# Two stores of a channel-attention kernel, split by partitions over two DMA queues

## The chip, the cores and the metric

The kernel runs on one core of one Trainium2 chip. The metric is the device time of one execution in microseconds. A profile is one execution taken by the hardware profiler; its span goes from the first to the last of the program's own instructions.

## What is computed

The input x is an image of 384 x 384 pixels with 384 channels in bf16 (113 MB). Each channel is averaged over the image, the average is multiplied by one weight and put through a sigmoid, and every pixel's channel is multiplied by the result:

```
g = jnp.einsum("bhwc->bc", x) / (H * W)
s = sigmoid(g * w1d[0])
return x * s[:, None, None, :]
```

So all of x must be read before the first byte of the result is known, and all of it is written. x does not fit into the core's memory: what doesn't stay has to be read twice.

## The kernel before

The pixels are dealt out as 1152 rows for each of 128 partitions; a row is one pixel's 384 channels (768 bytes) in every partition, so a row of all partitions is 96 KB. The tile `arena` holds the rows that are in the chip.

**First phase, to about 268 us.** Loads bring all rows into the arena (`load`, L235). TensorE sums each row over the partitions into one PSUM bank (`sum_rows`, `add_held`, L241 and L255). Some rows are only streamed through and are read again later. Others are kept: a few as they are, and most in groups that VectorE folds, four rows of bits into three (`fold`, `bits` L275, `join` L281), with a test by ScalarE (L312).

**The gap.** When the last row has landed and is summed, ScalarE takes the sigmoid (`s_bf`, L449) and copies it to PSUM (L453). In between, the DMA engines have nothing to do: nothing is left to load, and nothing can be stored.

**Second phase.** Rows that lie in the arena are multiplied by the scale on VectorE, three pieces of them on GpSimd (`scale`, L462), and stored (`store`, L472). The rows that were kept as they are come first, in a list: four times 2 rows at Y, four times 2 rows at T, then 6 rows at A + 26, 7 rows at A + 32, then 13 and more. Then folded groups are unfolded and scaled while streamed rows are loaded again (L235), scaled and stored. A load can start when the stores that read its place in the arena have landed.

**What sets the order.** Every DMA of x, load or store, is issued by SyncE (SP), one after the other, and SP waits at each until its turn may go. The order is written by a planner in the kernel, a loop over a model of time: it sends a store when VectorE should be through with its rows (`send`, then `waiting` and `store`), and issues a load when a large enough run of rows is idle. `Flow.add` records each step with what it reads and writes; `Flow.emit` turns that into semaphore waits (L106, L112) and gives each engine's DMAs 24 semaphores in turn (`LANES`). ScalarE's queue carries only the load of the weight. After the gap ScalarE copies rows that were parked in PSUM back into the arena (`copy_bank`, L387).

The first load after the gap fetches 21 rows into a run of the arena that starts in the rows named above, so it waits for their stores.

Of the kernel before, what the change touches and what calls it, by code (L numbers as in the profile page):

```python
# [127 lines left out]
def kernel(  # L128
# [11 lines left out]
    nc = tc.nc  # L140
    P = nc.NUM_PARTITIONS
# [18 lines left out]
    A = V + PAIR  # L160
# [27 lines left out]
    arena = pool.tile([P, ROWS, C], bf16, name="arena")  # L188
# [11 lines left out]
    of = out.rearrange("b h w c -> (b h w) c")  # L200

    def view(t, r0, n):
        return t[r0 * P : (r0 + n) * P, :].rearrange("(p r) c -> p r c", r=n)

    def rows(lo, n):
        return [("a", r) for r in range(lo, lo + n)]

    fl = Flow(nc, tc)
# [5 lines left out]
    STREAMED, KEPT = (0, N_STREAM), (N_STREAM, N_KEPT)  # L214
# [76 lines left out]
    def fold(k):  # L291
# [46 lines left out]
        reads=["ones", "w_bf"], writes=["bank0"],  # L338
# [4 lines left out]
        reads=["bank0"], writes=["w_sc"],  # L343
# [41 lines left out]
    def copy_bank(i, src, dst, reads, writes):  # L385
        fl.add(
            "ACT", lambda: nc.scalar.copy(dst.bitcast(u32), src.bitcast(u32)), reads=reads, writes=writes  # L387
        )

    for i, bk in enumerate(banks):  # L390
        lo, hi = i * BANK, min((i + 1) * BANK, PS * C)
# [51 lines left out]
    for a, n in S2 + [(U, 8)] + S3 + S1 + [(V, 8), (Y + 2, 6), (T + 6, 4), (T + 3, 3), (T + 1, 2), (T, 1)]:  # L443
# [6 lines left out]
        reads=["bank0", "w_sc"], writes=["s_bf"],  # L450
# [6 lines left out]
    def scale(a, n, eng="DVE", s=s_bf, after=()):  # L457
        v = arena[:, a : a + n, :]
        vec = nc.vector if eng == "DVE" else nc.gpsimd
        fl.add(  # L460
            eng,
            lambda: vec.tensor_tensor(  # L462
                out=v, in0=v, in1=s[:, None, :].to_broadcast([P, n, C]), op=Op.mult
            ),
            reads=rows(a, n) + ["s_bf" if s is s_bf else "bank0"], writes=rows(a, n), after=after,
        )

    def store(chunk, a, lo, hi):
        r0, n = chunk
        return fl.add(  # L470
            "SP",
            lambda: nc.sync.dma_start(out=view(of, r0, n)[:, lo:hi, :], in_=arena[:, a : a + hi - lo, :]),  # L472
            reads=rows(a, hi - lo), dma=True,
        )

    def unfold(k, first):

# [40 lines left out]
    def TT(n):  # L518
        return 0.15 + 0.2 * n
# [85 lines left out]
    def send(chunk, a, lo, hi, then, known=None):  # L605

        waiting.append((dve_at, hi - lo, then, chunk, a, lo, [] if known is None else known))

    def backlog():
        return sum(e[1] for e in moves) + ROW * sum(e[1] for e in waiting)  # L610
# [10 lines left out]
    def stored(a, n):  # L621

        def f():
            for i in range(a, a + n):
                for left in needed:
                    left.discard(("a", i))
                if not Y <= i < Y + 8 and not U <= i < U + 8 and not V <= i < V + 8:
                    idle[i] = True
        return f
# [30 lines left out]
    def start_group():  # L660

        if not line:
            return False
        g = line[0]
        column = home[g]
        if needed[column] or not free[column] or g == BANKED and (bank_at is None or now < bank_at[1]):
            return False
        line.popleft()
        free[column] = False
        a, q = GROUPS[g]  # L670
        if g == BANKED:
            a = bank_at[0]

        below = 0
        if column < 2 and g != COLUMNS[column][0]:
            below = GROUPS[COLUMNS[column][COLUMNS[column].index(g) - 1]][1]

        def part():
            release(a + below, sent - below)

        def done():
            nonlocal out_rows
            out_rows += 1
            free[column] = True
            release(a + max(below, sent), n_rows - max(below, sent))

        for k in of_group(g):
            turns.extend(step + (None,) for step in unfold(k, a))
        sent, n_rows = 0, 4 * q + (g == BANKED)
        if len(line) >= total - N_SPLIT and q == PAIR:  # L690

            f, t, _ = turns[-6]
            sent = 3 * PIECE
            turns[-6] = (f, t, lambda: send(KEPT, a, c_group[g], c_group[g] + sent, part, written))
        f, t, _ = turns[-1]
        turns[-1] = (f, t, lambda: send(KEPT, a + sent, c_group[g] + sent, c_group[g] + n_rows, done, written))
        return True

    while True:

        if dve_at <= now:
            ahead = backlog()
            can = bool(turns)
            if not can and not alongside and (ahead >= PENDING or not landed):
                can = start_group()
            if landed and (ahead < PENDING or not can):
                chunk, a, lo, n, end = landed.popleft()
                scale(a, n, s=s_ps if alongside and now else s_bf)
                dve_at = now + TT(n)
                since = (a, lo) if since is None else since  # L710
                if end or ahead < MERGE:
                    b, first = since
                    send(chunk, b, first, lo + n, stored(b, lo + n - first))
                    since = None
            elif can:
                f, t, then = turns.popleft()
                f()
                dve_at = now + t
                if then:
                    then()  # L720
        if alongside and alongside[0][0] <= now:
            _, chunk, a, lo, n = alongside.popleft()
            store(chunk, a, lo, lo + n)
            moves.append([now + LAT, n * ROW + PER_STORE, stored(a, n)])
        while waiting and waiting[0][0] <= now:
            _, n, then, chunk, a, lo, known = waiting.popleft()
            known.append(store(chunk, a, lo, lo + n))
            last_is_load = False
            moves.append([now + LAT, n * ROW + PER_STORE, then])
        if not asked and not line and not turns:  # L730
            verdict()
            asked = True
        if out_rows == total and not checked:
            checked = True
            fl.add("POOL", again, reads=["odd_i", "s_bf"], writes=rows(Y, N_OVER), after=written)
        while over and over[0][0] <= now:
            over.popleft()[1]()

        got = runs()
        if bank_at is None and len(line) <= total - BANKS_AT and got and max(got)[0] > PS * 4 // 3:  # L740
            a = max(got)[1]
            for i in range(a, a + PS * 4 // 3 + 1):
                idle[i] = False
            back = arena[:, a : a + PS, :].rearrange("p r c -> p (r c)")
            for i, bk in enumerate(banks):
                lo, hi = i * BANK, min((i + 1) * BANK, PS * C)
                copy_bank(i, bk[:, 0 : hi - lo], back[:, lo:hi], [("bank", i)], rows(a, PS))
            for i, (lo, hi, corner) in enumerate(corners):
                copy_bank(i, corner, arena[:, a + PS * 4 // 3, lo:hi], [("corner", i)], rows(a + PS * 4 // 3, 1))
            bank_at = (a, now + 5.0)  # L750
            got = runs()

        if got and todo < N_STREAM:
            n, a = max(got)
            n = min(n, CAP, N_STREAM - todo)
            ahead = backlog()

            queue = sum(e[1] for e in moves)
            turn = last_is_load or not todo or queue >= DEEP or queue < SHORT
            if turn and (todo or not landed and not waiting) and (n >= BIG or n == N_STREAM - todo or (ahead < LOW and n >= 8) or ahead < LAST):  # L760
                last_is_load = True
                load(STREAMED, a, todo, todo + n)
                for i in range(a, a + n):
                    idle[i] = False
                parts = [(STREAMED, a + e, todo + e, f - e, f == n) for e, f in split(n, PART)]
                todo += n
                moves.append([now + LAT, n * ROW + PER_LOAD, lambda parts=parts: landed.extend(parts)])

        if moves and moves[0][0] <= now:
            moves[0][1] -= DT  # L770
            if moves[0][1] <= 0:
                over.append((now + SEEN, moves.popleft()[2]))
        else:
            stall += DT
        if not (alongside or moves or waiting or over or landed or line or turns) and todo == N_STREAM:
            break
        now += DT
# [34 lines left out]
```

## Time and profile before

| What | us |
|---|---|
| Three runs | 720.52 to 720.86, median 720.71 |
| The profiled execution: its own time | 720.0 |
| Its span | 718.2 |
| VectorE busy | 494.8 (69%) |
| TensorE busy | 212.4 (30%) |
| ScalarE busy | 116.5 (16%) |
| GpSimd busy | 9.4 (1%) |
| Last row summed, sigmoid starts | 268.20 |
| First store issued | 269.40 |
| Store of 6 rows (576 KB) issued | 273.91 |
| Store of 7 rows (672 KB) issued | 275.38 |
| First load after the gap (2016 KB) issued | 282.53 |

The page gives the busy share of each engine in 40 equal slices of the span, and the share of the 16 DMA engines with the rate that they moved. A window asks the same for a stretch of one's own. The window counts a DMA packet by its start, so in a short window the share can be a little over 1. The chain of waits follows the work that ended last back in time. The list of DMA issues gives the median time from the issue of a DMA to its landing, that is to the last of its 16 completions.

### The profile page before, as it was taken

What the parts mean: (1) busy time and instruction counts of PE and PEld (TensorE: products, weight loads), DVE (VectorE), ACT (ScalarE), POOL (GpSimd) and SP (SyncE); (2) the same over time, 40 slices, a digit from 0 to 9 for tenths busy, and PEclk for the clock granted to TensorE, in tenths of its full rate; (3) what the DMA queues carried; (4) which work ended last, traced back from release to release, by engine and by line L of the source; (5) the groups of instructions that cost most, each with busy time, mean ns of one, the idle gap of its engine ahead of it and who ended that gap; (6) DMA issues with size and microseconds to landing.
All of it is one profiled execution on the core that took longest, in us unless ns stands there. A gap on an engine that the chain in (4) does not pass through costs nothing.

```text
span 718.2 us, 2075 instructions
## 1 busy us (share of the span) xinstructions
PE 212.4 (30%) x1202; PEld 0.3 (0%) x3; DVE 494.8 (69%) x475; ACT 116.5 (16%) x97; POOL 9.4 (1%) x7
## 2 busy tenths in 40 slices
PE   4678778898877770000000000000000000000000
PEld 0000000000000000000000000000000000000000
DVE  4600004787999819989999999899999795035910
ACT  3700003565777610001000000000000000000000
POOL 0000000000000005000000000000000000000000
PEclk9899999999999995555555555555555555555555
DMA  9999999999999989999999999999999999999997
GB/s 383 429 442 431 427 427 437 436 437 419 428 427 427 428 334 385 403 432 422 431 428 434 430 436 427 430 428 445 429 438 424 432 433 435 439 432 426 427 445 309
DMA packets 20893, 303.69 MB, mean 423 GB/s; under 512 B 2322, under 2 KB 3602, under 8 KB 6546
## 3 DMA queue, kind: packets, MB, share of 16 engines
q1 hardware_dynamic: 20880, 303.57, 99.0%
q8 instruction: 4, 0.07, 0.0%
q14 instruction: 7, 0.06, 0.0%
q10 hardware_dynamic: 2, 0.00, 0.0%
HBM read 190.32 MB, written 113.25 MB: 423 GB/s over the span
## 4 chain that ended last, share of the span: by engine, by line
DMA 63%; DVE 23%; PE 7%; ACT 1%; SPq 1%; issue 0%; another core or an unknown queue 0%; DVEq 0%
DMA arena<-in_x_dram 51%; DVE arena L462 17%; DMA out_dram<-arena 13%; PE bank L241 7%; DVE arena L275 3%; DVE arena L281 2%; ACT arena L312 1%; SPq L235 0%; SPq L472 0%; ACT s_bf L449 0%; SPq L112 0%; SPq L807 0%; DVEq L112 0%; SPq L106 0%
## 5 line engine op out<-in xcount | busy, mean ns | idle before, releaser
L462 DVE TENSOR_TENSOR arena<-arena,s_bf 128x1536 bf16<-128x1536 bf16 (+9 forms) x96 | 228.3, 2410 | 73.8 <-DMA arena<-in_x_dram 58.1
L275 DVE TENSOR_SCALAR arena<-arena 128x1536 uint16<-128x1536 uint16 (+2 forms) x247 | 145.2, 633 | 106.6 <-DMA arena<-in_x_dram 100.4
L241 PE MATMUL bank<-arena,ones 128*128 128x384 bf16 x1151 | 203.9, 338 | 46.8 <-DMA arena<-in_x_dram 46.7
L281 DVE TENSOR_TENSOR arena<-arena 128x1536 uint16<-128x1536 uint16 (+2 forms) x114 | 121.2, 1063 | 7.5 <-PE bank L241 4.5
L312 ACT ACTIVATE arena<-arena 128x3072 uint16<-128x3072 uint16 (+1 forms) x38 | 102.5, 2696 | 142.1 <-DVE arena L275 142.1
L539 PE MATMUL bank<-odd,ones 128*128 128x1 bf16 x1 | 0.2, 187 | 325.1 <-DVE odd L534 325.1
L387 ACT COPY arena<-bank 128x512 uint32<-128x512 uint32 (+2 forms) x8 | 4.2, 534 | 69.3 <-DMA out_dram<-arena 69.1
L462 POOL TENSOR_TENSOR arena<-arena,s_bf 128x1536 bf16<-128x1536 bf16 x3 | 9.2, 3105 | 268.8 <-ACT bank L453 268.8
L462 DVE TENSOR_TENSOR arena<-arena,bank 128x768 bf16<-128x768 bf16 (+4 forms) x12 | 12.3, 1095 | 0.0
L241 PE MATMUL bank<-s_bf,ones 128*128 128x384 bf16 x48 | 8.3, 326 | 0.0
L312 ACT ACTIVATION_READ_ACCUMULATOR arena<-arena 128x1 f32 x38 | 7.1, 186 | 0.0
L387 ACT COPY bank<-arena 128x512 uint32<-128x512 uint32 (+2 forms) x8 | 3.8, 528 | 0.0
L449 ACT ACTIVATE s_bf<-bank,w_sc 128x384 bf16<-128x384 f32 x1 | 0.6, 582 | 14.2 <-PE bank L241 14.2
L255 PE MATMUL bank<-arena,ones 128*128 128x384 bf16 x1 | 0.5, 477 | 7.0 <-DMA arena<-in_x_dram 7.0
L780 ACT ACT_TABLE_LOAD x1 | 1.3, 1283 | 0.7 <-PEq L796 0.7
L332 DVE MEMSET ones<- 128x128 bf16 x1 | 0.2, 165 | 1.1 <-SPq L106 1.1
L337 PE MATMUL bank<-w_bf,ones 1*128 1x1 bf16 x1 | 0.2, 180 | 2.2 <-DMA w_bf<-in_w1d_dram 2.2
L342 DVE TENSOR_SCALAR w_sc<-bank 128x1 f32<-128x1 f32 x1 | 0.2, 158 | 0.9 <-PE bank L337 0.9
L539 PEld LDWEIGHTS bank<-odd,ones 128*128 128x128 bf16 x1 | 0.1, 105 | 583.8 <-DVE odd L534 583.8
L543 DVE CAST odd_i<-bank 128x1 int32<-128x1 f32 x1 | 0.2, 158 | 0.3 <-PE bank L539 0.3
L453 ACT COPY bank<-s_bf 128x192 uint32<-128x192 uint32 x1 | 0.3, 323 | 0.0
L387 ACT COPY arena<-rest 128x64 uint32<-128x64 uint32 x1 | 0.2, 246 | 0.0
(10 smaller groups left out, 1.4 us busy)
## 6 DMA issues: line engine op xcount, KB each, us to landing
arena<-in_x_dram SPq DMA_DIRECT2D x14, 4608.0 KB, 35.1
arena<-in_x_dram SPq DMA_DIRECT2D x20, 1248.0 KB, 13.9
out_dram<-arena SPq DMA_DIRECT2D x7, 3072.0 KB, 30.1
arena<-in_x_dram SPq DMA_DIRECT2D x6, 3072.0 KB, 27.4
arena<-in_x_dram SPq DMA_DIRECT2D x7, 2304.0 KB, 19.6
out_dram<-arena SPq DMA_DIRECT2D x3, 4608.0 KB, 37.7
arena<-in_x_dram SPq DMA_DIRECT2D x3, 4512.0 KB, 36.1
out_dram<-arena SPq DMA_DIRECT2D x3, 4512.0 KB, 34.1
```

The lines of the kernel that those rows point to most:

```text
L241: return pe.add_instruction(mybir.InstMatmult(name=nc.get_next_instruction_name(), ins=[pe.lower_ap(rhs), pe.lower_ap(ones[:])], outs=[pe. ...
L255: return nc.tensor.matmul(acc, lhsT=ones[:], rhs=arena[:, i, :], start=first, stop=last)
L275: lambda: nc.vector.tensor_scalar(out=dst, in0=src, scalar1=s0, scalar2=s1, op0=op0, op1=op1),
L281: "DVE", lambda: nc.vector.tensor_tensor(out=dst, in0=a, in1=b, op=op), reads=reads, writes=writes
L312: lambda: nc.scalar.activation(out=y, in_=y, func=ACTF.Copy, accum_out=seen[:, 2 * k + i : 2 * k + i + 1]),
L332: fl.add("DVE", lambda: nc.vector.memset(ones[:], 1.0), writes=["ones"])
L387: "ACT", lambda: nc.scalar.copy(dst.bitcast(u32), src.bitcast(u32)), reads=reads, writes=writes
L449: lambda: nc.scalar.activation(out=s_bf[:], in_=acc, func=ACTF.Sigmoid, scale=w_sc[:, 0:1]),
L453: "ACT", lambda: nc.scalar.copy(s_ps.bitcast(u32), s_bf[:].bitcast(u32)), reads=["s_bf"], writes=["bank0"]
L462: lambda: vec.tensor_tensor(out=v, in0=v, in1=s[:, None, :].to_broadcast([P, n, C]), op=Op.mult),
L539: lambda: nc.tensor.matmul(votes, lhsT=ones[:], rhs=odd[:], start=True, stop=True),
L780: nc.scalar.preload_act_table(ACTF.Sigmoid)
```

## The change

The stores of the 6 rows at A + 26 and of the 7 rows at A + 32 are no longer one DMA each. SyncE stores partitions 0 to 95 of them; ScalarE's queue stores the other 32 in four DMAs, of partitions 96 to 109, 110 to 119, 120 to 125, and 126 to 127. All other stores go as before. The planner's model counts such a store as it did. The lines below `store` move down by 15, and `store` itself is now L482; on ScalarE the eight new issues stand between L453 and the copies from PSUM (L387 in both).

```diff
-    def store(chunk, a, lo, hi):
+    WHOLE, STAIRS = (P,), (96, 14, 10, 6, 2)
+    assert sum(STAIRS) == P
+
+    def store(chunk, a, lo, hi, blocks=WHOLE):
         r0, n = chunk
-        return fl.add(
-            "SP",
-            lambda: nc.sync.dma_start(out=view(of, r0, n)[:, lo:hi, :], in_=arena[:, a : a + hi - lo, :]),
-            reads=rows(a, hi - lo), dma=True,
-        )
+        sent, p0 = [], 0
+        for i, b in enumerate(blocks):
+            p = slice(p0, p0 + b)
+            queue = nc.scalar if i else nc.sync
+            sent.append(
+                fl.add(
+                    "ACT" if i else "SP",
+                    lambda p=p, queue=queue: queue.dma_start(
+                        out=view(of, r0, n)[p, lo:hi, :], in_=arena[p, a : a + hi - lo, :]
+                    ),
+                    reads=rows(a, hi - lo), dma=True,
+                )
+            )
+            p0 += b
+        return sent
...
-            known.append(store(chunk, a, lo, lo + n))
+            known.extend(store(chunk, a, lo, lo + n, STAIRS if chunk is KEPT and a in (A + 26, A + 32) else WHOLE))
```

The first load after the gap waits for all ten DMAs of these two stores now, where it waited for two: 14 semaphores in place of six.

## The prediction

> **What bounds the kernel now.** I read the 40 slices first, to see which engine is never idle, then the DMA queues, then the chain around the gap, then short windows of the DMA engines in the gap and at the end. The page:
>
> ```profile
> DMA  9999999999999989999999999999999999999997
> GB/s 383 429 442 431 427 427 437 436 437 419 428 427 427 428 334 385 403 432 422 431 428 434 430 436 427 430 428 445 429 438 424 432 433 435 439 432 426 427 445 309
> q1 hardware_dynamic: 20880, 303.57, 99.0%
> ```
>
> The 16 DMA engines are busy in every slice, at about 430 GB/s, so 26.9 GB/s each, and all on one queue, SP's. After the gap nothing but that stream matters: time is won or lost where an engine idles, where the packets of the engine that ends last get slower, or where that engine is given more of them. Windows of the gap and of the end (columns: window, length, PE, PEld, DVE, ACT, POOL, clock, DMA share, GB/s):
>
> ```profile
> 269.00:270.00 1.00, 0.00 (x0) 0.00 (x0) 1.00 (x3) 0.14 (x1) 0.79 (x1) 1.00 0.00 0
> 270.00:270.50 0.50, 0.00 (x0) 0.00 (x0) 0.50 (x2) 0.00 (x0) 0.50 (x1) 1.00 0.49 187
> ...
> 712.50:713.00 0.50, 0.00 (x0) 0.00 (x0) 0.00 (x0) 0.00 (x0) 0.00 (x0) 0.50 1.05 442
> 713.00:713.50 0.50, 0.00 (x0) 0.00 (x0) 0.00 (x0) 0.00 (x0) 0.00 (x0) 0.50 0.43 178
> 713.50:714.00 0.50, 0.00 (x0) 0.00 (x0) 0.00 (x0) 0.00 (x0) 0.00 (x0) 0.50 0.18 74
> 715.50:716.00 0.50, 0.00 (x0) 0.00 (x0) 0.00 (x0) 0.00 (x0) 0.00 (x0) 0.50 0.12 49
> 716.00:716.50 0.50, 0.00 (x0) 0.00 (x0) 0.00 (x0) 0.00 (x0) 0.00 (x0) 0.50 0.03 12
> ```
>
> The gap ends at about 270.25 (half of the window 270.0 to 270.5 is busy), with all engines starting together, 0.85 us after the first store is issued at 269.40. At the end they do not stop together: the share is full until 713.0, then seven engines' worth, three, two, until 716.3. So some engines are done **3.2 us** before the last one, and the last one sets the time. The page does not name the engines, so I can't see which ones are late.
>
> **The change, part by part.** The two stores, of 6 and 7 rows, are the 576 KB and the 672 KB one. The window 273.5 to 275 (queue summary, issues) holds the first:
>
> ```profile
> DMA packets 302, 0.61 MB, mean 408 GB/s; under 512 B 32, under 2 KB 174, under 8 KB 302
> out_dram<-arena SPq DMA_DIRECT2D x1, 576.0 KB, 3.2
> out_dram<-arena SPq DMA_DIRECT2D x1, 192.0 KB, 2.4
> ```
>
> (1) *Packets.* The 32 packets under 512 B are the completions of the two stores that end there: 16 a store, one an engine. So an engine moves 8 of a store's 128 partitions, one packet each. At 26.9 GB/s a packet of 6 rows (4608 B) takes 0.171 us, one of 7 rows (5376 B) 0.200 us: 0.371 us for a partition of both stores, and 8 x 0.371 = 3.0 us for both on each engine. After the change an engine has 6 partitions of the 96, and of each block at most one: 6 to 10 instead of 8. So an engine gets between -2 x 0.371 = -0.74 us and +0.74 us of work. The sum over the engines stays the same.
>
> (2) *The relief is cut short.* The next large store (1248 KB) is issued at 278.04, so its packets can start 0.85 us later, at 278.9. The store ahead of it, 384 KB issued at 275.75, lands 3.9 us later, at 279.65; the first small store's data began at 270.25, took 0.5 us, and landed at 271.3, so a landing is seen 0.5 us after the data, and this one's data ended at 279.15. An engine with less to do can gain 0.25 us and then waits for that issue. Relief is worth -0.25 us, a burden the full +0.74 us.
>
> (3) *Issues on ScalarE.* Eight more DMA issues there, at the 0.33 to 0.46 us that SP's take in this stretch: 2.6 to 3.7 us, from 273.9. Its timeline:
>
> ```profile
> 268.81 0.32 ACT L453 COPY bank<-s_bf 128x192 uint32<-128x192 uint32 x1
> 338.22 4.35 ACT L387 COPY arena<-bank 128x512 uint32<-128x512 uint32 x8 [69.08 <-DMA out_dram<-arena]
> ```
>
> Nothing stands behind them until 338.22, and that copy waits for a DMA: 60 us of cover, cost nothing. SP keeps one issue a store, with the same waits; neither VectorE nor GpSimd gets or loses an instruction.
>
> (4) *A wider wait on SP.* The first load after the gap (L235, 2016 KB) overwrites these rows. It waited for six stores and now waits for 14 DMAs, eight semaphores more. The chain around it:
>
> ```profile
> 281.57 0.33 SPq L472
> ...
> 281.95 0.02 SPq L112
> ...
> 282.53 11.22 DMA arena<-in_x_dram
> ```
>
> Six waits took from 281.90 to 282.53, about 0.1 us each, so eight more are 0.8 us at most. Behind them in SP stand this load and all later issues. The cover: the load lands 11.2 us after its issue, and its own bytes are 2016 KB / 430 GB/s = 4.8 us, with 0.85 us of start and 0.5 us of landing; so its packets queue for 5 us. Cost nothing, and 0.8 us if that queue were empty. The blocks themselves must land by 282.5 plus those 5 us; issued by 277, even 4.5 us late they do.
>
> (5) *Packets that share a path.* This no row of before shows: every transfer of x in it spans 128 partitions. Its stores run at 16 times one engine's rate, so there each engine has a way out of the arena of its own. A block of 14 neighbouring partitions, read by up to 14 engines at once, may not: the bounds are one engine on a path (no loss) and all 14 in turn on one. I take four, the middle of 1 and 14 by ratio (their geometric mean is 3.7). Then a packet of the blocks takes four times as long: 3 x 0.371 = 1.11 us more for both stores, in each of the blocks of 14, 10 and 6, and with two engines in turn 0.37 us in the block of 2. An engine that serves all four blocks loses 3 x 1.11 + 0.37 = 3.7 us, and with its two extra packets **4.45 us**. One that serves only the 14 gets -0.37 + 1.11 = +0.74 us. In the 96 partitions engines may meet on a path too: in pairs for all six packets it is 6 x 0.371 = 2.2 us more; I take nothing for it, since the other half of the engines would then be free of it, and keep the upper end.
>
> [...]
>
> **The sum.** If the engines with all four blocks are those that end first now, they eat up their 3.2 us: 4.45 - 3.2 = +1.25 us. If they are the last, +4.45 us. Not seeing which, I take the middle, **+2.8 us**. The profiled execution is 720.0 us (span 718.2 and 1.8 around it), so 722.8; the median of the runs shown is 720.71, 0.7 above it, so **723.5 us**.
>
> **The rivals.**
> - *Every engine keeps its own pace (not slower).* If a block's packets share nothing, (1) and (2) are all: from -0.25 us, where the engines that end last are spared, to +0.74 us, where they serve all blocks: 720.5 to 721.5. It decides if a 14-partition block moves at 14 times 26.9 GB/s. For it: no window of full-width DMA shows one engine slowing another. Against: nothing narrower was ever tried here. Chance 0.32.
> - *Out of step (faster).* Twice after the gap all engines slow together: the windows 286 to 288 move 280 and 339 GB/s, 297 to 299 move 359 and 290; against 430 that loses (150 + 91 + 71 + 140) / 430 = 1.1 us. If it is their lockstep out of the gap, a stagger might save it, and with 0.25 us of relief that is 1.35 us: 719.4. It decides if these windows come back to 430 GB/s. Against: later store-to-load turns in the slices show no loss, in step or not. Chance 0.04.
> - *The wait of (4) bares itself.* A block that lands after 287.5 holds all of SP. A load 3 us late is some 3 us for all engines: 724. Chance 0.04.
>
> **How the numbers follow.** Forecast 0.60, rivals 0.32, 0.04 and 0.04. A measurement here tells 0.2% (1.44 us) from no change. Of the forecast about 0.06 lies under 1.44 us (it begins at +1.25). Slower: 0.54 + 0.04 = 0.58; same: 0.32 + 0.06 + 0.02 (half of the out-of-step case, since 1.35 us is on the edge) = 0.40; faster: 0.02. The range starts at 720.3, which takes in the own-pace case, and ends at 726.0: 720.71 + 4.45 and 0.85 of the 2.2 us for pairs in the 96. The forecast alone has 722.0 to 726.0.
>
> **What would show it.** In the profile after, (5) is right if the windows 275 to 283 move clearly under 400 GB/s at full DMA share, with the landings of the 96-partition stores and of the blocks above 3.3 us; wrong if they keep 400 to 450. (2) shows as a share under 1 near 279. (4) is right if the 2016 KB load is issued by 283.3 and still lands near 293.7. The end shows which engines were late: a decay from 713 longer than 3.2 us means the late ones were loaded, a start of the decay later than 713 with the same end that the early ones were. The forecast is wrong if the blocks land in about 2 us each and the decay at the end ends where it ended before.

## The result and the profile after

The changed kernel is slower: 722.70 us (median of 7 runs) against 720.52 for the kernel before on the same chips, a ratio of 1.0033 with a 95% interval of 1.0019 to 1.0046, so 1.4 to 3.3 us. The profiled execution took 721.96 us, with a span of 720.2 us (718.2 before). ScalarE's queue on its page (packets, MB, share of the 16 engines):

```profile
q10 hardware_dynamic: 130, 0.32, 0.2%
```

All but 2 of its 130 packets are the blocks' (64 of data, 64 completions). The 40 slices of the page are too long to show where the time went. Windows of 2 us behind the gap can. The kernel before, then the one after (columns as in the prediction; the last two are DMA share and GB/s):

```profile
274.00:276.00 2.00, 0.00 (x0) 0.00 (x0) 2.00 (x2) 0.00 (x0) 2.00 (x2) 0.50 1.05 419
276.00:278.00 2.00, 0.00 (x0) 0.00 (x0) 2.00 (x2) 0.00 (x0) 2.00 (x1) 0.50 1.00 416
278.00:280.00 2.00, 0.00 (x0) 0.00 (x0) 2.00 (x3) 0.00 (x0) 0.44 (x1) 0.50 1.02 419
280.00:282.00 2.00, 0.00 (x0) 0.00 (x0) 2.00 (x3) 0.00 (x0) 0.00 (x0) 0.50 1.06 444
```

```profile
274.00:276.00 2.00, 0.00 (x0) 0.00 (x0) 2.00 (x2) 0.00 (x0) 2.00 (x2) 0.50 1.16 350
276.00:278.00 2.00, 0.00 (x0) 0.00 (x0) 2.00 (x2) 0.00 (x0) 2.00 (x1) 0.50 0.88 306
278.00:280.00 2.00, 0.00 (x0) 0.00 (x0) 2.00 (x2) 0.00 (x0) 0.34 (x1) 0.50 1.00 368
280.00:282.00 2.00, 0.00 (x0) 0.00 (x0) 2.00 (x3) 0.00 (x0) 0.00 (x0) 0.50 1.00 397
```

In three of the four windows the DMA engines count as fully busy and move less: the packets last longer. In the other, 276 to 278, they also stand still for a while (0.88). The four windows fall short by 69 + 110 + 51 + 47 GB/s for 2 us each; at 430 GB/s that is 1.3 us. Over the longer stretch from 268 to 312 us the engines moved 16.32 MB where they had moved 17.06, so they are 1.7 us behind, and their mean busy time is only 0.2 us less: nearly all of the loss is packets that last longer. Behind 312 the distance stays (1.6 us at 400). The landings agree: the two 96-partition stores landed after 4.4 and 4.5 us, where the whole stores took 3.2 and 3.3. The end, by windows of the kernel after:

```profile
713.00:713.50 0.50, 0.00 (x0) 0.00 (x0) 0.00 (x0) 0.00 (x0) 0.00 (x0) 0.50 1.03 436
...
714.50:715.00 0.50, 0.00 (x0) 0.00 (x0) 0.00 (x0) 0.00 (x0) 0.00 (x0) 0.50 0.39 160
...
718.00:718.50 0.50, 0.00 (x0) 0.00 (x0) 0.00 (x0) 0.00 (x0) 0.00 (x0) 0.50 0.03 12
```

Before, the share was 0.43 at 713.0 to 713.5; now it is full there and falls to 0.39 at 714.5. The first engines end more than a microsecond later, and the last packets start in 718.0 to 718.5 in place of 716.0 to 716.5, 2 us later. So of the 2.0 us in this execution 1.7 are lost in the mean of the 16 engines, and some 0.3 by the last one alone. How much each engine lost, a mean does not tell.

### The profile page after: what moved, and what is told of

It reads as the page before. It is cut to its first block, busy times and chain, and to the rows that moved or that the text cites. A ratio compares the mean times of both kernels' runs of the same rounds, so it can differ in the third digit from the quotient of the medians.

```text
span 720.2 us, 2091 instructions
## 1 busy us (share of the span) xinstructions
PE 213.7 (30%) x1202; PEld 0.3 (0%) x3; DVE 495.0 (69%) x475; ACT 116.5 (16%) x97; POOL 9.4 (1%) x7
## 2 busy tenths in 40 slices
DMA packets 20957, 303.70 MB, mean 422 GB/s; under 512 B 2386, under 2 KB 3666, under 8 KB 6610
## 4 chain that ended last, share of the span: by engine, by line
DMA 71%; DVE 16%; PE 7%; ACT 1%; SPq 0%; issue 0%; another core or an unknown queue 0%; DVEq 0%
DMA arena<-in_x_dram 50%; DMA out_dram<-arena 21%; DVE arena L462 13%; PE bank L241 7%; DVE arena L275 2%; DVE arena L281 1%; ACT arena L312 1%; SPq L235 0%; ACT s_bf L449 0%; SPq L482 0%; SPq L822 0%; DVEq L112 0%; SPq L112 0%; SPq L106 0%
## 5 line engine op out<-in xcount | busy, mean ns | idle before, releaser
L387 ACT COPY arena<-bank 128x512 uint32<-128x512 uint32 (+2 forms) x8 | 4.2, 534 | 71.9 <-DMA out_dram<-arena 71.7
L387 ACT COPY bank<-arena 128x512 uint32<-128x512 uint32 (+2 forms) x8 | 3.8, 528 | 0.0
L453 ACT COPY bank<-s_bf 128x192 uint32<-128x192 uint32 x1 | 0.3, 323 | 0.0
L387 ACT COPY arena<-rest 128x64 uint32<-128x64 uint32 x1 | 0.2, 244 | 0.0
## 6 DMA issues: line engine op xcount, KB each, us to landing
arena<-in_x_dram SPq DMA_DIRECT2D x20, 1248.0 KB, 13.9
```

The costliest lines, as they stand in the source:

```text
L453: "ACT", lambda: nc.scalar.copy(s_ps.bitcast(u32), s_bf[:].bitcast(u32)), reads=["s_bf"], writes=["bank0"]
```

## The experiments

The theories are: **shared path**, where engines that read neighbouring partitions take turns; **own pace**, where only the number of packets per engine counts; and **queue or wait**, where the second queue or the longer wait of the first load costs the time. Ratios stand against the kernel before on the same chip. The last two columns come from the traces, one execution each: how far the DMA engines are behind the kernel before at 312 us, by the bytes that they moved since 268 at 430 GB/s, and how much of that is time in which they stood idle (mean of the 16). The rest is packets that lasted longer.

| Run | us | Ratio (95% interval) | Behind, us | Of it idle |
|---|---|---|---|---|
| the change | 722.70 | 1.0033 (1.0019 to 1.0046) | 1.7 | 0.2 |
| act_whole | 720.34 | 1.0003 (0.9994 to 1.0012) | 0.0 | 0.0 |
| split_96_32 | 720.90 | 1.0008 (0.9999 to 1.0017) | 1.1 | 0.2 |
| one_store | 720.77 | 1.0007 (0.9998 to 1.0016) | 0.9 | 0.2 |
| one_block | 720.88 | 1.0010 (1.0001 to 1.0019) | 0.8 | 0.2 |
| step4_even | 721.19 | 1.0015 (1.0006 to 1.0024) | 0.5 | 0.4 |
| step4 | 721.35 | 1.0021 (1.0011 to 1.0030) | 1.9 | 1.5 |
| blocks_on_sp | 722.95 | 1.0041 (1.0027 to 1.0055) | 2.8 | 1.5 |
| first_6 | 724.62 | 1.0059 (1.0045 to 1.0073) | | |
| first_2 | 724.91 | 1.0068 (1.0054 to 1.0082) | | |

### Partitions alone

```diff
+    PATTERNS = [
+        slice(0, 128), slice(0, 96), slice(96, 128), slice(96, 110), slice(0, 118, 9),
+        slice(110, 120), slice(120, 126), slice(126, 128), slice(3, 128, 4), slice(0, 64),
+    ]
+    for i, p in enumerate(PATTERNS):
+        for j in range(REPS):
...
+                lambda p=p, r=r: nc.sync.dma_start(out=of[p, r : r + N, :], in_=arena[p, :, :]),
...
+            "DVE", lambda i=i: nc.vector.memset(mark[0:1, i : i + 1], 0.0),
+            reads=[("sent", i, j) for j in range(REPS)], writes=[("mark", i)],
```

> This kernel computes nothing: it stores a cleared arena, eight DMAs of 13 rows for each of ten choices of partitions, each choice alone and from SyncE's queue, with a small VectorE instruction behind each choice as a mark. One partition's packet of 13 rows takes 0.375 us in the profile before. If every engine keeps its own pace, the choices take, besides about 2 us of start and landing: 128 partitions 24 us, 96 18, 32 (the last ones) 6, 14 3, 14 at a step of 9 3, 10 3, 6 3, 2 3, 32 at a step of 4 6, 64 12. If four neighbouring partitions share a path: 128 24, 96 18 to 24, 32 12, 14 12, 14 at a step of 9 still 3, 10 12, 6 12, 2 6, 32 at a step of 4 6 to 12, 64 24.

The marks in its timeline; the number in brackets is how long VectorE waited, so how long the eight stores of one choice took (those of the first choice were issued from 3.70 on, so they took 25.7 us):

```profile
29.42 0.06 DVE L175 MEMSET mark<- 1x1 f32 x1 [25.76 <-DMA out_dram<-arena]
58.71 0.06 DVE L175 MEMSET mark<- 1x1 f32 x1 [29.22 <-DMA out_dram<-arena]
72.65 0.06 DVE L175 MEMSET mark<- 1x1 f32 x1 [13.89 <-DMA out_dram<-arena]
86.54 0.06 DVE L175 MEMSET mark<- 1x1 f32 x1 [13.83 <-DMA out_dram<-arena]
94.78 0.06 DVE L175 MEMSET mark<- 1x1 f32 x1 [8.18 <-DMA out_dram<-arena]
108.56 0.06 DVE L175 MEMSET mark<- 1x1 f32 x1 [13.72 <-DMA out_dram<-arena]
122.31 0.06 DVE L175 MEMSET mark<- 1x1 f32 x1 [13.69 <-DMA out_dram<-arena]
129.82 0.06 DVE L175 MEMSET mark<- 1x1 f32 x1 [7.45 <-DMA out_dram<-arena]
137.78 0.06 DVE L175 MEMSET mark<- 1x1 f32 x1 [7.90 <-DMA out_dram<-arena]
164.47 0.06 DVE L175 MEMSET mark<- 1x1 f32 x1 [26.63 <-DMA out_dram<-arena]
```

Lines 3, 4, 6 and 7 are the last 32 partitions, 14, 10 and 6 neighbours: 13.7 to 13.9 us each, the 12 us of four in turn with just under 2 us of start and landing, though the largest has five times the bytes of the smallest. Sixty-four neighbours (26.63) take about as long as all 128. Thirty-two at a step of 4 (7.90) keep own pace. The 96 take 29.2 us, longer than the 128 with a third more data, and 3 us above the upper end I expected. The 14 at a step of 9 took 8.2, where both theories had 3 and about 2; their eight issues alone span 6.58 us in the trace, so this choice is bound by its issues. It shows that 14 engines need not take 12 us, not what they need. The 2 partitions took 7.45, near the 6 and about 2 of a shared path; their issues span only 4.59 of it.

A rival has the same times: neighbours could be dealt to fewer engines, each at its own pace. The trace is against it. From 62 to 71 us, in the last 32 partitions, the 16 engines are busy for a share of 0.98 and move 201 GB/s; from 131 to 136, in the 32 at a step of 4, they are busy for 1.00 and move 415. From 111 to 120, the 6 neighbours keep 4.5 engines busy (0.28 of 16) at 36 GB/s, so 8 GB/s each. So it is not fewer engines, but longer packets: own pace is refuted for neighbours.

### Which engines end last

Both kernels with five tiny loads at the end of SyncE's queue:

```diff
+    for i, n in enumerate((2, 6, 10, 14, 16)):
...
+            lambda i=i, n=n: nc.sync.dma_start(out=rest[0:n, 16 * i : 16 * i + 16], in_=view(xf, 0, RPP)[0:n, i, 0:16]),
...
+            lambda i=i, n=n, copy=copy: copy(out=rest[0:n, 80 + i : 81 + i], in_=rest[0:n, 16 * i : 16 * i + 1]),
```

> The kernel before, with five tiny loads at the end of SyncE's queue, into 2, 6, 10, 14 and 16 partitions, each with a one-column copy that waits for it. If a load of n partitions goes to n engines, always the same first ones, the copy behind it starts when the last of those engines has come to its end. If the engines that serve all four blocks (the first two) are among the last now, the copy for 2 starts within 0.5 us of the last one, and the change should have cost more than 4 us; if they are among the first, it starts some 3 us before the last one.

> The changed kernel with the same five tiny loads and copies. By the shared path, engines with blocks fall back by up to 4.45 us against those with none: the copy for 2 partitions moves later by more than the copy for 16 does. By own pace alone it moves by 0.74 us at most. By a late first load on SyncE all five copies move by the same 2 us.

Timelines, the kernel before (720.13 us), then the changed one (723.50 us):

```profile
713.77 0.14 DVE L791 COPY rest<-rest 2x1 bf16<-2x1 bf16 x1 [29.16 <-DMA rest<-in_x_dram]
716.25 0.19 ACT L791 COPY rest<-rest 6x1 bf16<-6x1 bf16 x1 [373.56 <-DMA rest<-in_x_dram]
716.81 0.14 DVE L791 COPY rest<-rest 16x1 bf16<-16x1 bf16 x1 [0.23 <-DMA rest<-in_x_dram]
```

```profile
717.83 0.14 DVE L806 COPY rest<-rest 2x1 bf16<-2x1 bf16 x1 [30.35 <-DMA rest<-in_x_dram]
719.43 0.19 ACT L806 COPY rest<-rest 6x1 bf16<-6x1 bf16 x1 [373.21 <-DMA rest<-in_x_dram]
719.97 0.14 DVE L806 COPY rest<-rest 16x1 bf16<-16x1 bf16 x1 [0.22 <-DMA rest<-in_x_dram]
```

The load for 2 partitions lands 3 us ahead of the one for 16, the load for 6 only 0.56 us ahead. That a DMA of n partitions goes to n engines agrees with the completions: the page of the change counts 64 packets under 512 B more than that of the kernel before (2386 against 2322), one for each partition of its eight blocks. That they are always the same first ones is an assumption; no view names the engines. Under it the first two engines end early, and a late one is among the third to the sixth; that later ones are not later still is likely, since the loads for 10 and 14 follow at 0.2 us each, but not shown. With the change the copy for 2 moves by 4.06 us, the one for 6 by 3.18, the one for 16 by 3.16 (single executions; the changed one lies 0.8 us above its median, so the differences within it are what counts). Under the same assumption the first two engines fell back most, by 0.9 us more than the last ones, as the shared path has it. Own pace by itself (0.74 at most) can't move a copy by 3 us. A delay of all engines by the same time would move all copies alike; a difference of 0.9 us in one pair of executions speaks against it but does not exclude it with own pace on top. What excludes that are the partitions alone, above, and the packets below.

### Both stores whole, on the other queue

```diff
-    WHOLE, STAIRS = (P,), (96, 14, 10, 6, 2)
+    WHOLE, STAIRS = (P,), (0, P)
...
+            if not b:
+                continue
```

> Both stores whole, 128 partitions, from ScalarE's queue. By the shared path no engine meets another: 720.5, within 0.1% of before. If the second queue itself, or a DMA on it that the first load has to wait for, costs the time, this is slower by about the measured 2 us (0.3%).

No change. The second queue costs nothing by itself that these runs can tell (the interval ends at 0.12%), and neither does a first load that waits for DMAs of both queues.

### Where the parts go

96 and 32 partitions, then all five blocks on SyncE's queue:

```diff
-    WHOLE, STAIRS = (P,), (96, 14, 10, 6, 2)
+    WHOLE, STAIRS = (P,), (96, 32)
```

```diff
-            queue = nc.scalar if i else nc.sync
+            queue = nc.sync
...
-                    "ACT" if i else "SP",
+                    "SP",
```

> Both stores as 96 partitions by SyncE and the other 32 in one DMA by ScalarE's queue. Every engine has 6 + 2 = 8 packets, as before. Own pace or engine counts: 720.5, no change. Shared path: alone, eight stores of 96 partitions took 29.2 us and eight of the 32 took 13.9, so per store (29.2 - 2) / 8 + (13.9 - 2) / 8 = 4.9 us against 3.0 us for 128 partitions: up to 1.9 us slower, 721.3 to 722.4, less where the two queues use different paths at one time.

> The same five blocks, all from SyncE's queue. If the second queue (its turns with the first one in each engine, its slow issues) makes the cost, this is back at 720.5 to 721. Shared path: an engine takes the blocks in turn, 1.5 us for each of the 14, 10 and 6 by the runs alone, so the engines with three blocks are 3.4 + 4.5 - 3.0 = 4.9 us back at most: 722 to 725.5, no faster than the change.

The first is 0.08% slower, and its interval just takes in no change: the bound of 1.9 us was not reached. Its trace shows a loss all the same: from 276 to 278 and from 278 to 280 us it moves 333 and 351 GB/s at shares of 1.01 and 1.00, and it ends up 1.1 us behind. So the parts of 96 and 32 already lengthen packets, without any small block. That the two parts use different paths at one time, as the expectation allowed, is not shown. The second is at least as slow as the change, so it is not ScalarE's queue. Two of its windows:

```profile
278.00:280.00 2.00, 0.00 (x0) 0.00 (x0) 2.00 (x3) 0.00 (x0) 0.53 (x1) 0.50 0.81 237
280.00:282.00 2.00, 0.00 (x0) 0.00 (x0) 2.00 (x2) 0.00 (x0) 0.00 (x0) 0.50 0.77 299
```

Where the parts come one after the other in one queue, engines stand still as well: shares of 0.77 and 0.81, and 1.5 of 2.8 us are idle time. That these are the engines that serve no block is likely, but the share does not name them.

### The same counts from every fourth partition

```diff
+        if blocks is STAIRS:
+            cuts = [(slice(j, P, 4), 0) for j in range(3)]
+            for b in STAIRS[1:]:
+                cuts.append((slice(3 + 4 * p0, 3 + 4 * (p0 + b - 1) + 1, 4), 1))
+                p0 += b
...
+        for p, i in cuts:
```

The second of these runs has `STAIRS = (96, 32)`, one DMA in place of the four blocks.

> The same counts per engine as the change, from other partitions: three DMAs of every fourth partition (32 each) by SyncE, and the last set of 32 in blocks of 14, 10, 6 and 2 of every fourth partition by ScalarE's queue. Alone, eight DMAs of 32 partitions at a step of 4 took 7.9 us, own pace. Engine counts alone: as slow as the change, 722.7. Shared path: a block now lies on paths of its own, or two packets on one, so at most 0.37 + 3 x 0.37 = 1.5 us for engines with three blocks: 720.5 to 722, clearly below the change.

> As the one at a step of 4, but its last 32 partitions are one DMA by ScalarE's queue: 8 packets an engine, no path shared beyond what 128 partitions do. Shared path and engine counts both: 720.5, no change. If a store in parts costs in itself (more issues, more waits at the first load), it is slower by as much as the change.

Neither settles it by its time. By the shared path the first was to lie between 720.5 and 722, and it does (721.35), but its interval overlaps that of the change. The second was to show no change by either theory and is 0.15% slower. Six issues in place of two hold up SyncE; a window of step4, then of step4_even:

```profile
276.00:278.00 2.00, 0.00 (x0) 0.00 (x0) 2.00 (x2) 0.00 (x0) 2.00 (x1) 0.50 0.59 238
```

```profile
276.00:278.00 2.00, 0.00 (x0) 0.00 (x0) 2.00 (x2) 0.00 (x0) 2.00 (x1) 0.50 0.90 369
```

These lose mostly by empty engines (1.5 of 1.9 us and 0.4 of 0.5), where the change loses by long packets: seven issues of step4_even span 273.85 to 278.22, 0.62 us each, and one of 144 KB is only 0.34 us of work at 430 GB/s. The packets do tell the theories apart. ScalarE's queue in the window 273.5 to 287.5 of the change, of split_96_32, of step4, and of step4_even (packets, MB, share of 16 engines):

```profile
q10 hardware_dynamic: 128, 0.32, 10.2%
```

```profile
q10 hardware_dynamic: 96, 0.32, 8.3%
```

```profile
q10 hardware_dynamic: 128, 0.32, 6.9%
```

```profile
q10 hardware_dynamic: 96, 0.32, 5.6%
```

The same 64 packets of data took 10.2% x 16 x 14 us = 22.8 us in blocks of neighbours and 15.5 us in the same blocks at a step of 4. In one DMA they took 18.6 us as 32 neighbours and 12.5 us at a step of 4. Own pace is 64 x 0.186 = 11.9 us. So the packets of the change's blocks last 1.9 times as long on average as they need to, and with equal counts per engine neighbours take half as long again as partitions at a step of 4.

### Less of it

```diff
-    WHOLE, STAIRS = (P,), (96, 14, 10, 6, 2)
+    WHOLE, STAIRS = (P,), (112, 14, 2)
```

```diff
-            known.extend(store(chunk, a, lo, lo + n, STAIRS if chunk is KEPT and a in (A + 26, A + 32) else WHOLE))
+            known.extend(store(chunk, a, lo, lo + n, STAIRS if chunk is KEPT and a == A + 26 else WHOLE))
```

> Both stores as 112 partitions by SyncE and blocks of 14 and 2 by ScalarE's queue. The third to the sixth engine have 7 + 1 = 8 packets, as before, the first two have 9. Engine counts: no change, 720.2. Shared path: one block with four engines in turn is 1.11 us for the late engines in place of three, so a third of what the change costs them: 721 to 721.5.

> Only the store of 6 rows goes in parts. If the cost is by packet, 6 of 13 rows cost 6/13 of 2.4 us: 1.1 us, 721.3. If it is the first load's wait or the second queue's slow issues, most of the 2.4 us stays: 722 or more.

0.10% and 0.07%: a third and a fifth of the change's 0.33%. Which engines have 8 packets in the first run and which 9 is again an assumption, as with the tiny loads. Both lie near what packets and blocks would give in proportion, 0.11% and 0.15%, and the second's interval reaches past it. Both times are a little under what the shared path was to give (721 to 721.5, and 721.3). The queue or wait theory (722 or more for one store) is out.

### More work for the first engines

```diff
+    spare = nc.dram_tensor("spare", (2, 104 * C), bf16, kind="Internal").ap()
+    fl.add(
+        "ACT",
+        lambda: nc.scalar.dma_start(out=spare, in_=view(xf, 0, RPP)[0:2, 0:104, :].rearrange("p r c -> p (r c)")),
+        writes=["spare"], dma=True, after=[copied],
+    )
```

> The kernel before, both stores whole, with one more copy behind the gap on ScalarE's queue: two lines of 80 KB from the input to a spare place in memory, one line an engine, 79872 B / 26.9 GB/s = 3.0 us more work for two engines. The input and the result stay as they are. If the first two engines end 3 us before the last one, as the tiny loads at the end showed, the end does not move: 720.2 to 720.7. If they were among the last: 723.2.

> The same with six lines, so 3.0 us more for six engines. If the last engine is one of the third to the sixth, and each engine's work adds up, the end moves by the full 3.0 us: 723.2. If the last engine is a later one, it stays at 720.2.

Both expectations failed, and in a telling way: a copy on two engines costs 0.68% or 4.9 us, and one on six engines no more (0.59%). One term of them was too small: the copy was taken at 26.9 GB/s an engine, but from 269 to 285 us its packets make up 3.9% x 16 x 16 us = 10 us, so 5 us on each of the two engines in place of 3.0. (That a line goes to one engine agrees with the completions: 2 more packets under 512 B than before, 2324 against 2322, and 6 more, 2328, with six lines.) Windows of first_2 behind the gap, and two of SyncE's issues, the third and the fourth store (start, length of both):

```profile
272.00:274.00 2.00, 0.00 (x0) 0.00 (x0) 2.00 (x4) 0.00 (x0) 2.00 (x2) 0.60 0.05 20
274.00:275.50 1.50, 0.00 (x0) 0.00 (x0) 1.50 (x2) 0.00 (x0) 1.50 (x2) 0.50 0.06 27
```

```profile
270.27 5.73 SPq L479 DMA_DIRECT2D out_dram<-arena  x2
```

For 3.5 us the engines move nothing but the copy. The fourth store's issue begins at 270.74 and holds SyncE for 5.3 us, until 276.0, when the two engines are through with their copy (its completions come between 275.5 and 276.0). So here SyncE's queue took only a few DMAs ahead of its slowest engines, and as these are short (192 KB, 0.45 us each), two engines that are a few microseconds late stopped all 16. Which engine is last at the end these two runs can't tell.

## Why the prediction was right

**Size and side.** 723.5 was forecast, 722.7 came; +2.8 us against +2.2 by the medians.

That neighbouring partitions slow each other's packets, as (5) has it, is shown (alone, 13.9 us for 32 neighbours and 7.9 for 32 at a step of 4), and the signs that the prediction named for it came: under 400 GB/s at full share (350 and 368), and landings above 3.3 us (4.4 and 4.5). That the size came so near is in part luck.

**(1) and the own-pace rival.** The packets per engine could make 0.74 us at most, and the lower bound of the interval is 1.4. The rival fell, and the packets' own times are against it as well.

**(2)** The relief of -0.25 us for engines with fewer packets did not show: the share stays at 1.00 from 278 to 280, and no run ended earlier than the kernel before.

**(3)** The issues were to take 2.6 to 3.7 us. They took 8.0 us, the last one issued at 280.74:

```profile
273.81 8.02 ACTq L482 DMA_DIRECT2D out_dram<-arena  x8
```

ScalarE's next work is the copy from PSUM at 340.70, so the cover was there and it cost nothing there. It did cost cover in (4).

**(4)** The load was to be issued by 283.3. It went out at 286.59, since the last block was late (the last packet of ScalarE's queue starts between 286.0 and 286.5), and landed 9.4 us later:

```profile
286.59 1.53 SPq L235 DMA_DIRECT2D arena<-in_x_dram  x2
...
arena<-in_x_dram SPq DMA_DIRECT2D x1, 2016.0 KB, 9.4
```

The issue was 4 us late where 0.8 were thought the most. Its own bytes with start and landing are 4.8 + 0.85 + 0.5 = 6.2 us, so of the 5 us of queue ahead of it 3.2 us were left, and the engines stayed full while SyncE waited (1.05 from 284 to 286). The cover held for the engines, but the load was to land near 293.7 and landed at 296.0, and VectorE waited 2.8 us for it where it had waited 0.5. From 290 to 302 the stream falls another 0.5 us behind, from 1.2 to 1.7. Whether the late load makes that is not shown; so "cost nothing" is not shown either. The rival, some 3 us for all engines by this wait, is out: 1.2 us were lost before 282, and no more than 0.5 behind the load.

**(5)** This is the step that carries the forecast. Four in turn is what neighbours measured alone (12 us in place of 3), with most of the block's engines busy meanwhile (4.5 of 6). In the change the blocks' packets last 1.9 times their own pace, not four times; why less, no run shows. In the probe the copy for 2 partitions moved by 4.06 us, near the 4.45 worked out for an engine with all four blocks, but the one for 16 moved by 3.16 too, so only 0.9 us is the first one's alone. The four was my estimate, the middle of two bounds; what the runs showed for it is 13.7 to 13.9 us for 6, 10, 14 and 32 partitions alike. That the same engines serve all four blocks no run shows, nor that engines meet in pairs in the 96 and half of them would be free of it.

Two more terms were off. The first: nothing was taken for the 96 partitions, and alone they take 29.2 us where own pace with start and landing would be 20 us, so 9.2 / 8 = 1.15 us a store of 13 rows. Beside the other 32 it shows as the 1.1 us by which split_96_32 falls behind, though only 0.08% in its time. The second is what the sum was made of: the middle of +1.25 and +4.45 was taken, since the late engines were not known. If a tiny load and a block of n both go to the first n engines, which no view shows, the first two are early and a late one is among the third to the sixth, which serve three blocks each. By the terms of (5) such an engine loses 3 x 1.11 + 0.37 = 3.7 us, and then +1.25 was never the lower end. Too much for the blocks, nothing for the 96 and a middle of two cases that may not have been the ones at hand came out near 2.2 us by luck; and most of the measured loss, 1.7 us, is one in the mean of all engines, not of a worst one.

**The stagger rival.** Slow windows came again (298 to 300 moves 245 GB/s after, 346 before); nothing was gained.

Two things stay open. One is how the longer packets divide between the small blocks and the parts of 96: the parts of 96 and 32 alone make 1.1 of the 1.7 us, but by one execution each. The other is how a loss in the mean of the engines passes on to the last one: first_2 shows that SyncE's issue can wait for the slowest engines, and in the change no view tells the engines apart.

## What to carry to other kernels

In these runs the engines fell behind where a store was split into parts of neighbours (1.7 us in the change, 1.1 in split_96_32): alone, eight stores of six neighbours took as long (13.7 us) as eight of 32 (13.9), and 32 at a step of 4 took 7.9. Parts spread evenly still cost their issues (step4_even, 0.15%). So count both before splitting. To shift load between DMA engines with short DMAs can cost more than it brings where one queue feeds all engines: in first_2 two engines that fell behind held the issue of the next DMA for the rest for 5.3 us, and the kernel took 0.68% longer. To see where a loss arises, add up the bytes that the engines moved since a common point, and their busy time: the first tells how far they are behind (1.7 us here), the second whether they stood idle (0.2 us of it) or their packets lasted longer. And when each engine's finish matters, tiny loads at the end of the queue, into 2, 6, 10 and so on partitions, show how far apart parts of the engines end (the copies for 2 and for 16 started 3.0 us apart), though not which engines they are.

## What was not expected of the hardware

The DMA of 96 neighbouring partitions is slower than that of 128 with a third more data: 29.2 against 25.7 us for eight of them. Thirty-two partitions at a step of 4 take 7.9 us where 32 neighbours take 13.9. And a copy on another queue that kept two of 16 engines busy stood in the way of SyncE's issue for 5.3 us, and for 3.5 us of that the other 14 had nothing to do (20 and 27 GB/s at a DMA share of 0.05 and 0.06).
